# A tuned attention and two-layer kernel: three more quarters of the first layer by seven products, an order written out, and wider fillers

## The chip, the cores and the metric

The kernel runs on one core of a Trainium2 chip. A core has a matrix engine (PE, with its weight loads, PEld), VectorE (DVE), ScalarE (ACT), GpSimd (POOL) and a queue engine (SP) that only issues transfers. Each engine runs its instructions in the order in which they were written; across engines they wait for one another by semaphores. The metric is device time in microseconds (us), lower is better.

## The reference

Attention in chunks of 64 tokens over 8 batches, 8 heads, 576 tokens and 64 dimensions a head, then two layers over the 4608 tokens with a leaky rectifier in between:

```python
scores = scale * np.matmul(q_c, k_c.transpose(0, 1, 2, 4, 3))   # chunks of 64 x 64
scores = scores - np.max(scores, axis=-1, keepdims=True)
attn = np.exp(scores)
attn = attn / (np.sum(attn, axis=-1, keepdims=True) + 1e-09)
out = np.matmul(attn, v_c)
x = out.transpose(0, 2, 1, 3).reshape(4608, 512)
h = x @ w_in                      # 512 x 2048
g = np.maximum(0.01 * h, h)
return (g @ w_out).astype(np.float32)   # 2048 x 512
```

## The kernel before

Tokens go through attention in 36 groups u of 128 tokens (two chunks for all heads). The steps of a group, by the letter that names them in the code:

- `arrive`: POOL issues the loads of q and k, which cast to f16 on the way (`load_rows`, L93).
- `t`: from group 10 on SP issues transposes of q and k by DMA (L428, L431), and POOL copies q into its place QZ, in two halves (`p`, L444). Before group 10 PE transposes them (`pe_t`, L404, L409).
- `s`: PE multiplies q and k (tile Sp, L451). `m`, `b`: DVE takes the maximum and subtracts it. `x`: ACT takes the exponential (L471). `z`, `n`: DVE sums, and DVE or POOL divides (tile en, L487).
- `d`: SP issues the transpose of en by DMA (tile et, L506). In the groups below 8 and in a few others PE transposes it (`e`, L495) and DVE or ACT copies it (`d2`).
- `v`: PE multiplies et by v (tile xp, L517). `a`: ACT copies xp into xT (L530).

The two layers work on 12 blocks of tokens, four of 128 and eight of 512 (`BLOCKS`). In the last eight the second layer is done by Strassen's scheme as Winograd has it: seven products of half size in place of eight, steps `m2` (tiles oA, oB, oC, L371), with sums made by DVE (`sf`, `wf`). In blocks 6 to 11 so is part of the first layer, counted in quarters of a block: `FAST` says how many of a block's four quarters. A quarter by seven products is the PE steps `f` with numbers 1 to 7 (`in_product`, L323, tiles hA, hB, hC), sums of the inputs on DVE (`xf`, tile XF, once for a block), three copies on ACT (`d`, `u2`, `u3`, L199), two additions on DVE (`+u2`, `+u3`, L235) and four activations on ACT (`g..`, L196). A plain quarter is 32 matmuls (`mm1`, L185, tile hT) and four activations on ACT. In blocks 6 and 7 the scheme works on 256 tokens at a time (`UNIT`), so that its matmuls are of 128 columns; in blocks 8 to 11 on 512 with 256 columns.

The order of all steps is made while the program is built. `run()` is a list scheduler: at each point it takes, of the steps that can begin soonest by its own account of durations, latencies, DMA queues, PSUM banks and temporary tiles, the one with the lowest key. `TUNE` shifts the keys of single steps, and `ON` says which engine does a step that several could. Where PE would stand idle ahead of a step in the first 40 us, `run()` puts fillers in, matmuls whose results nobody reads (`idle`, L532): each 128 columns of the identity with itself.

The first q and k come over the queues of SP and ACT as f32 (tiles q_f and k_f) and are cast by DVE and ACT (`cast_q`, `cast_k`). All other loads are issued by POOL, in the order of `front()` and of the groups; POOL makes the identity behind its first loads.

The lines that call the two functions in question:

```python
    second_fast(LAST, place)
    run()
```

## Time and profile before

| | |
|---|---|
| time, median of 3 runs | 277.74 us (276.58 to 278.91) |
| span of the profiled execution | 273.8 us (the page gives no other time of it) |
| matmuls hT, 256 and 128 columns | 96 and 768 |
| matmuls of seven products, first layer | 784 |
| fillers | 86 |

The page's timeline rows read: start and length in us, engine, line, operation, tile written and tiles read, shapes, count, and in brackets the idle time just ahead and what ended it. A group's row has its count, then busy time and the mean of one in ns, then the idle time ahead of them. A row of stretches has from and to, the length, and busy time of PE, PEld, DVE, ACT and POOL with the number of instructions, then the clock, the DMA share and GB/s. Where matmuls follow one another their rows overlap, since a matmul's end is modelled; what one costs is seen from the start of the next. A line "DMA to landing" gives the least, the median and the greatest time from issue to landing of the transfers in the stretch that was asked for.

### The profile page before, as it was taken

What the parts mean: (1) busy time and instruction counts of PE and PEld (TensorE: products, weight loads), DVE (VectorE), ACT (ScalarE), POOL (GpSimd) and SP (SyncE); (2) the same over time, 40 slices, a digit from 0 to 9 for tenths busy, and PEclk for the clock granted to TensorE, in tenths of its full rate; (3) what the DMA queues carried; (4) which work ended last, traced back from release to release, by engine and by line L of the source; (5) the groups of instructions that cost most, each with busy time, mean ns of one, the idle gap of its engine ahead of it and who ended that gap; (6) DMA issues with size and microseconds to landing.
All of it is one profiled execution on the core that took longest, in us unless ns stands there. A gap on an engine that the chain in (4) does not pass through costs nothing.

```text
span 273.8 us, 8229 instructions
## 1 busy us (share of the span) xinstructions
PE 263.2 (96%) x3406; PEld 238.2 (87%) x3406; DVE 208.2 (76%) x375; ACT 193.9 (71%) x359; POOL 158.9 (58%) x198
## 2 busy tenths in 40 slices
PE   1999999999999999999999999999999999999995
PEld 1889578799999999999999999899999989888884
DVE  5895285789978898899788999897879865831671
ACT  6588947778475644999796369978866896378721
POOL 8999783967898959587758778657351000000000
PEclk9999999999999999999999999999999999999999
DMA  9999999999999999999999999999954100220233
GB/s 134 154 191 183 182 176 176 155 173 217 151 158 152 120 143 208 170 144 234 154 155 121 136 140 247 133 186 197 136 84 151 43 19 2 77 79 0 79 115 116
DMA packets 162004, 38.27 MB, mean 140 GB/s; under 512 B 153008, under 2 KB 157616, under 8 KB 161968
## 3 DMA queue, kind: packets, MB, share of 16 engines
q0 software_dynamic: 114384, 18.09, 97.0%
q1 hardware_dynamic: 46544, 19.41, 42.2%
q8 instruction: 26, 0.43, 0.6%
q10 hardware_dynamic: 1040, 0.26, 0.4%
q14 instruction: 10, 0.08, 0.2%
HBM read 36.70 MB, written 9.44 MB: 169 GB/s over the span
## 4 chain that ended last, share of the span: by engine, by line
PE 90%; ACT 3%; DMA 3%; POOL 2%; issue 1%; DVE 0%; POOLq 0%
PE oA L371 20%; PE hT L185 17%; PE hA L323 14%; PE oC L371 10%; PE hC L323 7%; PE oP L210 5%; PE oB L371 5%; PE hB L323 3%; PE Sp L451 3%; PE xp L517 3%; DMA q_in<-in_q_dram 3%; PE tpe L495 1%; PE idle L535 1%; ACT gT L196 1%; ACT xT L530 1%; PE qp L404 1%
## 5 line engine op out<-in xcount | busy, mean ns | idle before, releaser
L371 PEld LDWEIGHTS <-gT 128*128 128x128 f16 x640 | 61.1, 98 | 6.6
L185 PE MATMUL hT<-xT,w_inT 128*128 128x128 f16 (+1 forms) x864 | 58.6, 225 | 0.1
L185 PEld LDWEIGHTS <-w_inT 128*128 128x128 f16 x864 | 53.1, 98 | 2.0 <-issue 0.4
L444 POOL COPY QZ<-QT 64x512 f16<-64x512 f16 x52 | 36.6, 705 | 20.0 <-DMA QT<-q_in 13.1
L196 ACT ACTIVATE gT<-hT 128x512 f16<-128x512 f32 x60 | 35.1, 599 | 15.9 <-PE hT L185 15.6
L235 DVE TENSOR_TENSOR tmp<-hC,tmp 128x512 f32<-128x512 f32 x42 | 27.9, 678 | 16.6 <-PE hC L323 8.3
L487 POOL TENSOR_TENSOR en<-ex,zi 128x512 f16<-128x512 f16 x22 | 23.8, 1083 | 26.8 <-DVE zi L481 12.3
L323 PEld LDWEIGHTS <-VF 128*128 128x128 f16 x448 | 34.5, 98 | 2.4
L93 POOL DMA_DIRECT2D q_in<-in_q_dram x39 | 33.8, 871 | 4.5 <-DMA w_outT<-in_moe_w_out_dram 1.8
L93 POOL DMA_DIRECT2D k_in<-in_k_dram x39 | 33.5, 863 | 1.2 <-DMA VB<-in_v_dram 0.8
L461 DVE TENSOR_REDUCE mx<-Sp 128x8 f32<-128x512 f32 x36 | 24.6, 684 | 10.3 <-PE Sp L451 10.2
L371 PE MATMUL oA<-WF,gT 128*128 128x256 f16 x256 | 32.2, 273 | 0.0
L199 ACT ACTIVATE tmp<-hA 128x512 f32<-128x512 f32 x42 | 24.3, 602 | 6.8 <-PE hA L323 6.8
L196 ACT ACTIVATE gT<-tmp 128x512 f16<-128x512 f32 x42 | 26.4, 634 | 3.7 <-DVE tmp L235 3.6
L323 PEld LDWEIGHTS <-w_inT 128*128 128x128 f16 x336 | 26.2, 98 | 1.9
L471 ACT ACTIVATE ex<-sh 128x512 f16<-128x512 f32 x36 | 22.8, 633 | 7.0 <-DVE sh L465 6.8
L371 PEld LDWEIGHTS <-S 128*128 128x128 f16 x256 | 24.6, 98 | 2.8
L477 DVE TENSOR_REDUCE z<-ex 128x8 f32<-128x512 f16 x36 | 24.3, 676 | 3.3 <-ACT ex L471 3.2
L530 ACT ACTIVATE xT<-xp 128x512 f16<-128x512 f32 x36 | 21.4, 597 | 7.6 <-PE xp L517 7.4
L465 DVE TENSOR_TENSOR sh<-Sp,mx 128x512 f32<-128x512 f32 x36 | 24.5, 681 | 0.6
L323 PE MATMUL hA<-XF,VF 128*128 128x128 f16 (+1 forms) x224 | 24.7, 246 | 0.0
L199 ACT ACTIVATE tmp<-oA 128x512 f32<-128x512 f32 (+1 forms) x27 | 14.9, 552 | 11.7 <-PE oA L371 11.6
(76 smaller groups left out, 478.7 us busy)
## 6 DMA issues: line engine op xcount, KB each, us to landing
out_dram<-osb SPq DMA_DIRECT2D x14, 512.0 KB, 5.2
VB<-in_v_dram POOLq DMA_DIRECT2D x14, 288.0 KB, 9.1
q_in<-in_q_dram POOLq DMA_DIRECT2D x31, 128.0 KB, 8.3
k_in<-in_k_dram POOLq DMA_DIRECT2D x31, 128.0 KB, 8.4
w_inT<-in_moe_w_in_dram POOLq DMA_DIRECT2D x8, 256.0 KB, 7.5
w_outT<-in_moe_w_out_dram POOLq DMA_DIRECT2D x4, 512.0 KB, 9.0
out_dram<-osb SPq DMA_DIRECT2D x6, 256.0 KB, 5.5
v_t<-in_v_dram POOLq DMA_DIRECT2D x4, 128.0 KB, 7.0
```

The source lines that it names most:

```text
L93: nc.gpsimd.dma_start(out=t[a - u * G:z - u * G], in_=src[b, :, r:r + z - a, :].rearrange("h p d -> p h d"))
L185: nc.tensor.matmul(out=hT[:, i, :], lhsT=w_inT[:, t, fc * 128:(fc + 1) * 128], rhs=xT[:, t, r0 % RING:r0 % RING + tb], start=(i == 0 and t ...
L196: nc.scalar.activation(out=to, in_=of, func=AFT.Prelu, bias=0.0, scale=1.0, alpha=0.01)
L199: nc.scalar.activation(out=to, in_=of, func=AFT.Copy, bias=0.0, scale=1.0)
L235: (nc.vector if e == "dve" else nc.gpsimd).tensor_tensor(out=to, in0=a, in1=b, op=ALU.add)
L323: nc.tensor.matmul(out=PA[key][:, c, :], lhsT=w[:, t, fc * 128:(fc + 1) * 128], rhs=x[:, t, :], start=(m in (1, 5) and c == 0 and t == 0), ...
L371: nc.tensor.matmul(out=to, lhsT=lhs[:, fc, p * 128:(p + 1) * 128], rhs=rhs[:, fc, :], start=(fresh and fc == 0), stop=(fc == HB - 1), skip ...
L444: nc.gpsimd.tensor_copy(out=QZ[u % NQZ][part, :, :, s, :], in_=QT[u][part].rearrange("p i (e t) -> p i e t", e=2))
L461: nc.vector.tensor_reduce(out=MX[u], in_=SP[u], axis=AXL.X, op=ALU.max)
L465: nc.vector.tensor_tensor(out=SH[u], in0=SP.pop(u), in1=MX.pop(u).unsqueeze(2).to_broadcast((128, 8, CH)), op=ALU.subtract)
L477: nc.vector.tensor_reduce(out=z, in_=E[u], axis=AXL.X, op=ALU.add)
L530: nc.scalar.activation(out=xT[:, :, at:at + G], in_=xp, func=AFT.Copy, bias=0.0, scale=1.0)
```

## The change

Four things:

1. `FAST` goes from 4, 3, 4, 2, 4, 4 to 4 in each of blocks 6 to 11: 24 quarters of the first layer by seven products instead of 21. The three are one of block 7 and two of block 9.
2. The scheduler goes. In its place `ORDER` lists all 1406 steps by number, with the fillers ahead of a step (how many, in which bank) and the PSUM banks and temporary tiles that the step takes. `TUNE` goes with it. The first third of the list is the order that the scheduler made (113 steps on PE, 98 on ACT, 95 on DVE and 84 on POOL, with the same fillers' places for the most part); behind it the order is another on every engine.
3. `ON` is written out for all steps. Three divisions `n` change engines: group 23 from POOL to DVE, 28 and 33 from DVE to POOL.
4. Fillers are of 512 columns on a tile of ones. DVE sets the tile (a part of XF, which is not yet in use) ahead of everything else that it does. In units of 128 columns there are 112 in place of 86. 21 of them stand ahead of PE's first step now.

```diff
-    FAST = {6: 4, 7: 3, 8: 4, 9: 2, 10: 4, 11: 4}
+    FAST = {6: 4, 7: 4, 8: 4, 9: 4, 10: 4, 11: 4}
...
+    ones = XF[0][:, 0].rearrange("p t n -> p (t n)")
+    nc.vector.memset(ones, 1.0)
     one = sbp.tile([128, 1], FP16, name="one")
     nc.vector.memset(one, 0.0)
...
     def idle(n, tag):
-        t = bank([128, 4, 128], "idle", tag)
-        for i in range(n):
-            nc.tensor.matmul(out=t[:, i % 4, :], lhsT=ident, rhs=ident, start=True, stop=True)
+        t = bank([128, 512], "idle", tag)
+        while n:
+            w = min(n, 4) * 128
+            nc.tensor.matmul(out=t[:, :w], lhsT=ones[:, :128], rhs=ones[:, :w], start=True, stop=True)
+            n -= w // 128
...
     def run():
-        now = {e: 0.0 for e in LAT}
-        now.update(pe=3.8, act=2.6, dve=0.95, pool=1.2, sp=1.3)
...
-        return order
+        for i, fill, *slots in ORDER:
+            s = steps[i]
+            if fill:
+                idle(fill[0], BANKS[fill[1]])
+            for h, slot in zip(s.take, slots):
+                h.slot = BANKS[slot] if h.pool == "bank" else slot
             s.emit()
...
-    TUNE = {('v', 5): (-8, 0.5), ('e', 6): (2, 0.5), ('a', 4): (0, 0.3), ('arrive', 26, 0): (4, 0.8),
...
+    ORDER = [
+        (55, 0), (0, 0), (56, 0), (62, 0), (1, 0), (59, 0), (60, 0), (64, 0), (61, 0), (2, 0), (57, 0), (63, 0), (65, 0), (3, 0), (66, 0), (4, 0), (52, 0), (5, 0),
+        (54, 0), (53, 0), (6, 0), (86, (21, 0), 0), (83, 0, 1), (7, 0), (87, 0), (112, 0, 2), (84, 0), (115, 0, 3), (8, 0), (114, 0), (85, 0), (113, 0), (116, 0),
...
```

The estimates of how long the weights' loads take (`load` in `front()`) change too; with the order written out, no instruction depends on them.

The fillers on PE, in units of 128 columns: before, 4 ahead of Sp of group 0, 40 and 8 ahead of the transposes of q of groups 2 and 3, 15 ahead of Sp of group 2, 19 ahead of the transpose of en of group 1. Now 21 ahead of the first step, 3 ahead of Sp of group 0, 36 and 7 ahead of the same transposes of q, 7 ahead of the transpose of en of group 0, 23 ahead of that of group 1, 9 and 6 ahead of xp of groups 0 and 1.

Two places show how the order moves. ACT around 82 to 91 us, before: ex are the exponentials of groups 13, 14 and 15, xT<-xp is the copy behind xp of group 11, gT<-hT are activations of block 5.

```order
L471 ACTIVATE ex_1890<-sh_1870 128x512
L196 ACTIVATE gT_1631<-hT_1873 128x4x128
L196 ACTIVATE gT_1631<-hT_1902 128x4x128
L196 ACTIVATE gT_1631<-hT_1923 128x4x128
L196 ACTIVATE gT_1631<-hT_1948 128x4x128
L471 ACTIVATE ex_1984<-sh_1968 128x512
L199 ACTIVATE tmp_2010<-oA_1970 128x512
L530 ACTIVATE xT_68<-xp_2014 128x4x128
L471 ACTIVATE ex_2063<-sh_2037 128x512
```

ACT at the same place now, from the exponential of group 13 to that of group 15:

```order
L473 ACTIVATE ex_1842<-sh_1820 128x512
L198 ACTIVATE gT_1578<-hT_1844 128x4x128
L198 ACTIVATE gT_1578<-hT_1868 128x4x128
L198 ACTIVATE gT_1578<-hT_1899 128x4x128
L532 ACTIVATE xT_68<-xp_1923 128x4x128
L198 ACTIVATE gT_1578<-hT_1933 128x4x128
L473 ACTIVATE ex_2021<-sh_1995 128x512
L198 ACTIVATE gT_1578<-hT_2000 128x4x128
L473 ACTIVATE ex_2049<-sh_2017 128x512
```

The copy behind xp of group 11 stands ahead of the fourth activation and of the exponential of group 14 now, as xp itself stands earlier on PE.

POOL from 166 to 177 us, before: q_in_3662 takes q of groups 32 and 33, q_in_3835 that of 34 and 35; QZ<-QT_3536 are the two copies of q of group 29 and QZ<-QT_3640 those of group 30, en are divisions.

```order
L93 DMA q_in_3662<-in_q_dram 128x8x64
L93 DMA k_in_3681<-in_k_dram 128x8x64
L93 DMA q_in_3662<-in_q_dram 128x8x64
L93 DMA k_in_3726<-in_k_dram 128x8x64
L444 COPY QZ_65<-QT_3536 64x8x64
L487 TENSOR_TENSOR en_3777<-ex_3633,zi_3749 128x512
L444 COPY QZ_65<-QT_3536 64x8x64
L487 TENSOR_TENSOR en_3807<-ex_3724,zi_3775 128x512
L93 DMA q_in_3835<-in_q_dram 128x8x64
L444 COPY QZ_65<-QT_3640 64x8x64 x2
```

POOL at the same place now: q_in_3831 takes q of groups 32 and 33, q_in_3568 (whose first half was loaded earlier) that of 34 and 35; QT_3577, QT_3658 and QT_3696 are groups 29, 30 and 31.

```order
L93 DMA k_in_3671<-in_k_dram 128x8x64
L446 COPY QZ_65<-QT_3577 64x8x64 x2
L489 TENSOR_TENSOR en_3735<-ex_3619,zi_3713 128x512
L489 TENSOR_TENSOR en_3788<-ex_3701,zi_3761 128x512
L446 COPY QZ_65<-QT_3658 64x8x64 x2
L93 DMA q_in_3831<-in_q_dram 128x8x64
L489 TENSOR_TENSOR en_3845<-ex_3786,zi_3808 128x512
L446 COPY QZ_65<-QT_3696 64x8x64
L489 TENSOR_TENSOR en_3933<-ex_3864,zi_3889 128x512
L446 COPY QZ_65<-QT_3696 64x8x64
L93 DMA q_in_3831<-in_q_dram 128x8x64
L93 DMA q_in_3568<-in_q_dram 128x8x64
```

The loads of q of groups 32 and 33 stand behind the copies of groups 30 and 31 now; those of k stay ahead of the copies of group 29.

On SP the store of one half of block 6's output stood ahead of the transpose of en of group 26 and stands behind it now. On PE three groups of eight hT matmuls of block 9 and one of product 3 of block 7 (tile oC) stood between the transpose of en of group 27 and xp of group 26 and are gone or behind it; and the sums `xf` of block 9 need the products of block 8 to be done, as they did before.

More of the change, by code (lines that the diff above doesn't have):

```diff
@@ L846, in front @@
                 for m in range(2):
-                    load(("Q", n[0], m), 0.62, lambda a=n[0], m=m: load_w_in(a, m), 1750 if n[0] == 0 else 1580)
+                    load(("Q", n[0], m), 0.62, lambda a=n[0], m=m: load_w_in(a, m), 1560)
             else:
                 load(("P", n[0]), 1.0, lambda a=n[0]: load_w_out(a), 2930)
-        for n, more in ((1, 500), (4, 700)) if arrivals[0].name[0] != "Q" else ((0, 1300), (1, -200)):
-            arrivals[n].dmas = [(p + more / len(arrivals[n].dmas), y) for p, y in arrivals[n].dmas]
         for x in arrivals:
```

182 lines of the change are left out of this document (11 added, 171 removed), and 108 rows, old and new, of tables (ON, ORDER).

## The prediction

> **What bounds the kernel now.** I read the page's busy shares and its chain first, then the waits of TensorE (PE), then busy time by stretch, and last the timeline of the places that the change touches.
>
> ```profile
> span 273.8 us, 8229 instructions
> PE 263.2 (96%) x3406; PEld 238.2 (87%) x3406; DVE 208.2 (76%) x375; ACT 193.9 (71%) x359; POOL 158.9 (58%) x198
> ...
> PE 90%; ACT 3%; DMA 3%; POOL 2%; issue 1%; DVE 0%; POOLq 0%
> ```
> ```profile
> PE kp L409 <- POOL ident masks.py:199: 6.0, 1, 6.0
> PE qp L404 <- DMA q_in<-in_q_dram: 0.4, 1, 0.4
> PE tpe L495 <- ACT gT L196: 0.3, 1, 0.3
> PE xp L517 <- POOL VB L120: 0.2, 1, 0.2
> ```
> ```profile
> 18.35:270.45 252.10, 251.62 (x3246) 227.45 (x3242) 193.99 (x342) 181.74 (x337) 142.27 (x171) 1.00 1.41 139
> ```
> The waits are all that PE ever waited for; their columns are the total, the times and the longest. Three of the four end before 18.35 us. From there to the last matmul PE is idle for 252.10 - 251.62 = 0.48 us. So the time is the point where PE's dense work begins, plus its own work, plus a tail. A change can win by giving PE less work or an earlier start, and any wait that it puts into the dense stretch is paid in full. The span is 273.8 us and the page gives no time beside it; the median of the runs, 277.74, is 3.9 above it. I take these 3.9 as unchanged and make the sum on the median.
>
> **The three quarters.** The work itself, from the chain (start, time, what):
>
> ```profile
> 107.84 0.89 PE hA L323 x16
> ...
> 127.14 0.87 PE hT L185 x8
> ```
> A matmul of 256 columns costs 0.87/8 = 0.109 us, one of 128 costs 0.89/16 = 0.0556. A plain quarter of the first layer is 32 matmuls of 256 columns, 3.48 us. As seven products it is 28 of 256 columns in block 9 (3.05 us) and 56 of 128 in block 7 (3.12 us), whose unit is 256 tokens. Two quarters of block 9 and one of block 7 change: 3 x 3.48 = 10.44 goes, 2 x 3.05 + 3.12 = 9.22 comes. PE has 1.2 us less to do, all of it on the path. That is the first term: -1.2.
>
> Each changed quarter also has seven copies and activations on ScalarE (ACT) in place of four, and two more additions on VectorE (DVE):
>
> ```profile
> L196 ACT ACTIVATE gT<-hT 128x512 f16<-128x512 f32 x60 | 35.1, 599 | 15.9 <-PE hT L185 15.6
> ...
> L235 DVE TENSOR_TENSOR tmp<-hC,tmp 128x512 f32<-128x512 f32 x42 | 27.9, 678 | 16.6 <-PE hC L323 8.3 <-ACT tmp L199 8.3
> L196 ACT ACTIVATE gT<-tmp 128x512 f16<-128x512 f32 x42 | 26.4, 634 | 3.7 <-DVE tmp L235 3.6
> ...
> L199 ACT ACTIVATE hB<-hA 128x512 f32<-128x512 f32 x21 | 12.0, 588 | 8.0 <-PE hA L323 7.7
> ```
> ```profile
> 117.00:139.00 22.00, 22.00 (x351) 21.02 (x349) 19.63 (x40) 20.11 (x39) 16.68 (x21) 1.00 1.86 175
> ...
> 169.00:196.00 27.00, 27.00 (x307) 24.46 (x305) 23.68 (x44) 23.70 (x45) 15.96 (x20) 1.00 1.90 181
> ```
> Four evictions of 599 ns are 2.4 us, seven of 588 to 634 are 4.1 to 4.4: ACT gains 1.9 us a quarter, DVE 2 x 0.68 = 1.4. Around block 7 (first row; the columns after PE and its weight loads are DVE, ACT, POOL) ACT goes from 20.1 to 22.0 of 22 us. Around block 9 it goes from 23.7 to 27.4, in a stretch that shrinks from 27 to 26.1. There ACT has 1.3 us too much, which must lie over into the next block. The copies for which PE waits (d, u2, u3) can run ahead of the activations that nobody needs yet, so I book zero, and keep +1.3 for the range. That is also what it costs if the cover is gone. What two operations win there isn't excluded, but PE was idle for nothing there, so there is no gain below zero.
>
> **The fillers and the front.** The first 113 PE steps, up to about 81 us, and those of ACT, DVE and POOL beside them, keep their order; only the fillers differ.
>
> ```profile
> 3.29 0.48 DVE L555 MEMSET QZ<- 128x512 uint32 x1
> ...
> 4.63 0.43 DVE L538 CAST q_in<-q_f 128x512 f16<-128x512 f32 x1 [0.86 <-DMA q_f<-in_q_dram]
> ```
> ```profile
> 9.66 3.11 PE L535 MATMUL idle<-ident 128*128 128x128 f16 x40
> 13.12 0.40 PE L404 MATMUL qp<-ident,q_in 128*128 128x128 f16 x4 [0.35 <-DMA q_in<-in_q_dram]
> ...
> 14.46 1.00 PE L535 MATMUL idle<-ident 128*128 128x128 f16 x15
> ...
> 15.75 1.23 PE L535 MATMUL idle<-ident 128*128 128x128 f16 x19
> ...
> 18.11 0.41 PE L517 MATMUL xp<-et,VB 128*128 128x64 f16 x8 [0.24 <-POOL VB L120]
> ```
> ```profile
> 16.79 1.27 POOL L120 COPY VB<-v_t 64x256 f16<-64x256 f16 x3
> ```
> The memset of the ones is no longer than the 0.48 us of the one shown; DVE waits 0.86 us for the first q right behind it, so it is hidden, and costs that rest if the q came earlier. Fillers are counted in 128 columns: 86 before, 112 now. The first 21 run while PE waited for the identity (the 6.0 us among the waits). The 36 ahead of the landing of q at 13.1 us are 4 fewer. Between there and 18.35 stand 52 against 42, about 52 x 0.0556 = 2.9 us by the warm rate. Where do they end? The last xp before the dense work waits for POOL's copies of v, 16.79 + 1.27 = 18.06, and no order on POOL changes there. The 10 more units cost 0.6 us, and about as much goes because Sp of group 2 has no fillers ahead of it any more. So the dense start stays at 18.35: term zero. Bounds: -0.5, all idle time of the dense stretch, and +0.6, the added units if POOL's cover went.
>
> What clock do these matmuls have? The 40 fillers run 3.11/40 = 0.078 us apiece, between 0.0556 and about twice that, and the 15 at 14.46 already 0.067 with the drain. PE reaches its full rate among the 40. The Trainium skill ("TensorE: Matmul & The Clock Gate", Part 1) says that the array runs at half clock until about 3.4 us of sustained work, counted in a window that runs freely, and Part 4 adds that transposes don't count as work. By that rule the early fillers, some 2 us and then a wait, need not open the gate by themselves; the trace agrees in that PE, begun at 5.96 with transposes, was slow until it had run fillers for a while.
>
> **The new order behind 81 us.** Three places are tight: where PE takes the transposed weights of attention (xp), or q (Sp), sooner than before.
>
> ```profile
> 82.37 1.19 SPq L506 DMA_TRANSPOSE et<-en  x1
> ...
> DMA to landing us min/median/max: 7.0/7.0/7.0
> ...
> 90.68 0.40 PE L517 MATMUL xp<-et,VB 128*128 128x64 f16 x8
> ```
> First, xp of group 11. Its transpose is issued at 82.4 and lands 7.0 later, at 89.4; its POOL step and all ahead of that keep their place, and ahead of it on SP only two transposes change places. One group of 16 hT matmuls (0.89) and one of 8 oA (0.87) that stood ahead of xp now stand behind it: PE is there 1.76 us earlier, at 88.9. Behind it on PE waits everything. That is a new wait of 0.5 us, the second term: +0.5 (bounds 0, if the transpose gets through faster, and 1.0).
>
> ```profile
> 172.75 7.05 SPq L506 DMA_TRANSPOSE et<-en  x2
> ...
> DMA to landing us min/median/max: 8.8/8.8/8.8
> ...
> 183.34 0.40 PE L517 MATMUL xp<-et,VB 128*128 128x64 f16 x8
> ```
> Second, xp of group 26: its transpose lands at 172.75 + 8.8 = 181.6. Three hT groups and one oC group (4 x 0.87) that stood ahead of it are gone or behind it, and with what block 7 saved PE is there 3.9 us earlier, at 179.5. Left alone that is 2.1 us of waiting. But the normalisation of this group stands earlier on DVE, and an output store that was ahead of the transpose on SP now stands behind it. I book zero and keep +2.1: a wait at one such place pushes the later ones back and isn't added to theirs, so the +0.5 of group 11 is inside it.
>
> ```profile
> 165.92 0.95 POOL L93 DMA_DIRECT2D q_in<-in_q_dram  x1
> ...
> 175.47 1.27 POOL L444 COPY QZ<-QT 64x512 f16<-64x512 f16 x2
> ...
> 183.76 0.94 POOL L93 DMA_DIRECT2D q_in<-in_q_dram  x1
> ...
> DMA to landing us min/median/max: 10.0/11.6/12.6
> ...
> DMA to landing us min/median/max: 5.3/5.3/5.3
> ...
> DMA to landing us min/median/max: 5.9/5.9/5.9
> ...
> 193.90 0.40 PE L451 MATMUL Sp<-KT,QZ 128*128 128x64 f16 x8
> ```
> Third, Sp of group 32, at 193.9 and now 1.25 us earlier, 192.65. The load of its q was issued at 165.9; now POOL issues it behind the copies of group 30, which end at 176.7. From there: the load, 5.3 (issued alone, as the one at 183.8 was, the second landing row) to 10.0 (least of the burst of four from 165.9, the first), the transpose, 5.9 (its own, the third) to 8.8 (the one of group 26), and POOL's copies, 1.3. That is 189.2 to 196.8, so from 3.4 us to spare to 4.1 late. The load is now nearer to the one issued alone, so I book zero.
>
> The tail is the same products of the last block in nearly the same order: zero. Sum: 277.74 - 1.2 + 0.5 = 277.0 us.
>
> **The rivals.**
> - Late weights. Group 26 keeps the landing of before, and PE waits 2.1 us in place of 0.5: 277.74 - 1.2 + 2.1 = 278.6. For it: the transposes of the row above take 7 to 8.8 us, and xp moved earlier than its supply at several groups. Against it: what stands ahead of it was moved too. ACT's 1.3 us too much around block 9 would give 277.8 and lies on the way to it.
> - Slower by q of group 32. With 10.0 and 8.8 PE waits 4.1 us: 277.74 - 1.2 + 4.1 = 280.6. It decides from 14.65 us for load and transpose together; each us above that is lost.
> - Nothing waits, and the last 0.5 us of idle time goes too: 277.74 - 1.2 - 0.5 = 276.0. For it: counted in the two orders, PE has 0.87 us of other work or more between any product and the next one that needs its copy, the shortest that before has too.
> - The clock comes late: the array stays at half rate past 13.1 us, because the first fillers are followed by a wait. Worked out from rows, at twice 0.0556: 52 units are 5.8 us, eight groups of four such are 3.6, so dense work begins at 22.5 instead of 18.35: 277.74 - 1.2 + 4.1 = 280.6. Against it: before reached the full rate by 13 us with less work ahead. (The Trainium skill's rule above, of "TensorE: Matmul & The Clock Gate", is what would do it.)
>
> **How the numbers follow.** The forecast, 277.0, gets 0.54 (its own range 276.2 to 277.9); late weights 0.18, q of group 32 0.14 (from 278.7 to 280.6), nothing waits 0.10, the clock 0.04. One measurement of this kernel tells about 1% from no change (the runs lie from 276.58 to 278.91): under 274.96 is faster, over 280.52 slower. Even the best case ends within 1%; only the scatter of the runs, 1.2 below the median, gets it under: 0.05. Slower takes most of the clock, half of q and a little of late weights: 0.13. The rest, 0.82, is within 1%. The range goes from the best case less that scatter, 274.9, to 279.7, the middle of the q case; about 0.17 lies outside.
>
> **What would show it.** Matmuls hT fall from 864 to 768, idle from 86 to 31. The last xp ahead of dense work still waits for POOL, and dense work begins by 18.4. PE's waits show xp at about 89 with half a microsecond on SP's transpose, and no Sp beyond 190 that waits for QZ. ACT is over 98% busy around block 7. Wrong would be: waits of PE on ACT in blocks 7 or 9, dense work that begins past 19, or PE's idle time in the dense stretch over 2 us.

## The result and the profile after

| | before | after |
|---|---|---|
| time, median | 277.71 us (275.08 to 280.17, 20 runs) | 278.50 us (277.29 to 282.67, 20 runs) |
| ratio to before | | 1.0053 [1.0028, 1.0078] |
| span of the profiled execution | 273.8 us | 276.0 us (its time 277.82) |

The change makes the kernel slower by half a per cent. Here and below a ratio leaves out executions that took over 1.5% more than the fastest of their kernel, while a median is of all, so the two can differ. It is worth being clear at once about two executions that are not alike: the span of 276.0 us belongs to a time of 277.82, 1.8 us more than the span. By the same 1.8 the execution of before with its span of 273.8 took about 275.6, two microseconds under the median of its kernel. The trace that the prediction was worked out from is one of the quickest of before. The spans on record say the same without this estimate: of the 154 executions of before that ran beside the experiments, the median span is 275.9 us, and nine are at 273.8 or less.

The page of after, first the busy times by engine, then the shares of the chain that ended last:

```profile
span 276.0 us, 8186 instructions
...
PE 264.9 (96%) x3367; PEld 234.4 (85%) x3367; DVE 214.4 (78%) x381; ACT 197.0 (71%) x368; POOL 157.3 (57%) x199
...
PE 83%; DMA 8%; ACT 3%; DVE 2%; POOL 2%; issue 1%; DVEq 0%; POOLq 0%
```

PE carries the chain as before, but DMA has 8% of it. The waits of PE in after (what PE waited in and the line, what for; total, times, longest in us); the first two and that of qp end ahead of the dense stretch:

```profile
PE kp L411 <- POOL ident masks.py:199: 2.1, 1, 2.1
PE idle L538 <- DVE zeros L157: 1.5, 1, 1.5
PE xp L519 <- DMA et<-en: 1.0, 1, 1.0
PE qp L406 <- DMA q_in<-in_q_dram: 0.9, 1, 0.9
PE hA L325 <- DVE XF L285: 0.4, 1, 0.4
PE tpe L497 <- ACT gT L198: 0.3, 1, 0.3
PE Sp L453 <- DMA KT<-k_in: 0.3, 1, 0.3
PE hC L325 <- ACT gT L198: 0.2, 1, 0.2
```

The stretches of after, with the columns that were explained for before:

```profile
18.35:82.00 63.65, 63.32 (x985) 54.97 (x982) 47.02 (x85) 47.57 (x85) 50.37 (x62) 1.00 1.98 171
82.00:117.00 35.00, 33.47 (x483) 31.03 (x482) 30.62 (x51) 19.65 (x37) 24.84 (x32) 1.00 1.95 161
117.00:139.00 22.00, 21.59 (x361) 20.56 (x357) 21.20 (x43) 20.16 (x39) 13.99 (x17) 1.00 1.95 170
139.00:169.00 30.00, 29.93 (x387) 27.58 (x385) 27.73 (x46) 21.00 (x40) 24.39 (x30) 1.00 2.29 146
169.00:196.00 27.00, 27.00 (x311) 24.29 (x310) 24.39 (x47) 24.84 (x49) 15.62 (x20) 1.00 1.47 163
196.00:272.00 76.00, 76.00 (x754) 68.25 (x750) 48.83 (x79) 51.52 (x100) 11.02 (x14) 1.00 0.35 79
```

PE stands idle for 1.53 us between 82 and 117 (35.00 against 33.47) and for 0.41 between 117 and 139. The largest piece is xp of group 14, which asks 1.75 us sooner in PE's work than before, while its weights are divided later (on DVE a sum for the second layer, a sum of the weights and all of group 15 come first) and SP sends group 15's transpose ahead of it. The view by tile of et between 96 and 108 us shows the two transposes, 15 at 97.5 and 14 at 98.8, the wait of 1.0, and the time from issue to landing:

```profile
L508 SPq DMA_TRANSPOSE et<-en x2: 1254/1547/1840, 97.5 to 98.8; - x2
...
  DMA et<-en: 1.0, 1
...
DMA to landing us min/median/max: 7.7/7.9/8.0
```

To put every profile of this study on one scale, the span is cut in four. Dense: from the start to the first matmul of the dense work. Work: all matmuls from there on, by the distance from one start to the next where nothing waits, 29.4, 55.6, 109.1 and 215.5 ns for 64, 128, 256 and 512 columns. Waits: what the distances between starts have above that, each over 15 ns. Rest: the remainder, nearly all of it behind the last matmul.

| profile | span | dense | work | waits | rest |
|---|---|---|---|---|---|
| before, the one shown | 273.8 | 18.35 | 250.38 | 1.23 | 3.81 |
| before, again (`b_again`) | 274.2 | 18.47 | 250.38 | 1.56 | 3.79 |
| after | 276.0 | 18.37 | 249.13 | 4.18 | 4.29 |
| after, again (`a_again`) | 277.1 | 18.58 | 249.13 | 5.15 | 4.27 |

So from the one shown to after: -1.25 of work, as forecast, +0.02 of the front, +2.95 of waits and +0.48 at the end, together +2.2 us. The waits are the term to explain: before's trace had 1.23, and the time of an ordinary run of before leaves room for 3.3 (277.7 less 1.8 is a span of 275.9, less 18.37, 250.38 and 3.8).

### The profile page after: what moved, and what is told of

Same layout as the page of the kernel before. It is cut to its first block, busy times and chain, and to the rows that moved or that the text cites. A ratio compares the mean times of both kernels' runs of the same rounds, so it can differ in the third digit from the quotient of the medians.

```text
span 276.0 us, 8186 instructions
## 1 busy us (share of the span) xinstructions
PE 264.9 (96%) x3367; PEld 234.4 (85%) x3367; DVE 214.4 (78%) x381; ACT 197.0 (71%) x368; POOL 157.3 (57%) x199
## 2 busy tenths in 40 slices
DMA packets 162005, 38.28 MB, mean 139 GB/s; under 512 B 153008, under 2 KB 157616, under 8 KB 161968
## 4 chain that ended last, share of the span: by engine, by line
PE 83%; DMA 8%; ACT 3%; DVE 2%; POOL 2%; issue 1%; DVEq 0%; POOLq 0%
PE oA L373 18%; PE hA L325 14%; PE hT L187 14%; PE oC L373 9%; PE hC L325 7%; DMA et<-en 5%; PE oP L212 5%; PE oB L373 4%; PE hB L325 3%; PE xp L519 3%; PE Sp L453 3%; DMA q_in<-in_q_dram 2%; PE tpe L497 1%; ACT gT L198 1%; PE idle L538 1%; POOL q_in L93 1%
## 5 line engine op out<-in xcount | busy, mean ns | idle before, releaser
L446 POOL COPY QZ<-QT 64x512 f16<-64x512 f16 x52 | 34.5, 665 | 28.7 <-DMA QT<-q_in 21.2
L187 PE MATMUL hT<-xT,w_inT 128*128 128x128 f16 x768 | 47.1, 219 | 0.0
L237 DVE TENSOR_TENSOR tmp<-hC,tmp 128x512 f32<-128x512 f32 x48 | 32.3, 684 | 15.9 <-ACT tmp L201 8.9
L187 PEld LDWEIGHTS <-w_inT 128*128 128x128 f16 x768 | 44.0, 98 | 0.6
L325 PEld LDWEIGHTS <-VF 128*128 128x128 f16 x512 | 39.9, 98 | 3.7 <-issue 0.9
L198 ACT ACTIVATE gT<-hT 128x512 f16<-128x512 f32 x48 | 27.9, 600 | 14.2 <-PE hT L187 14.0
L489 POOL TENSOR_TENSOR en<-ex,zi 128x512 f16<-128x512 f16 x23 | 24.6, 1068 | 20.1 <-ACT tmp L201 10.6
L201 ACT ACTIVATE tmp<-hA 128x512 f32<-128x512 f32 x48 | 28.1, 601 | 6.9 <-PE hA L325 6.6
L325 PEld LDWEIGHTS <-w_inT 128*128 128x128 f16 x384 | 30.3, 98 | 2.2
L198 ACT ACTIVATE gT<-tmp 128x512 f16<-128x512 f32 x48 | 29.9, 633 | 2.6 <-DVE tmp L237 2.6
L325 PE MATMUL hA<-XF,VF 128*128 128x128 f16 (+1 forms) x256 | 28.3, 246 | 0.4 <-DVE XF L285 0.4
```

Of the source, the lines that this page charges most:

```text
L187: nc.tensor.matmul(out=hT[:, i, :], lhsT=w_inT[:, t, fc * 128:(fc + 1) * 128], rhs=xT[:, t, r0 % RING:r0 % RING + tb], start=(i == 0 and t ...
L198: nc.scalar.activation(out=to, in_=of, func=AFT.Prelu, bias=0.0, scale=1.0, alpha=0.01)
L201: nc.scalar.activation(out=to, in_=of, func=AFT.Copy, bias=0.0, scale=1.0)
L237: (nc.vector if e == "dve" else nc.gpsimd).tensor_tensor(out=to, in0=a, in1=b, op=ALU.add)
L325: nc.tensor.matmul(out=PA[key][:, c, :], lhsT=w[:, t, fc * 128:(fc + 1) * 128], rhs=x[:, t, :], start=(m in (1, 5) and c == 0 and t == 0), ...
L446: nc.gpsimd.tensor_copy(out=QZ[u % NQZ][part, :, :, s, :], in_=QT[u][part].rearrange("p i (e t) -> p i e t", e=2))
```

## The experiments

Eighteen kernels, in five batches; each batch has its own runs of before on the same chip, and ratios are to those. The theories, as the expectations number them:

- T1: the new order loses the time, at places where PE takes transposed data sooner.
- T2: the three quarters load DVE and ACT so that PE waits for them, whatever the order.
- T3: the fillers cost it.
- T4: the execution of before that was profiled was a lucky one.
- T5: fewer filler instructions shift the fetches of PE's program, and the gaps that they make in DMA traffic, against the loads.
- T6: DMA supply is a second bound up to 200 us, so that PE work taken out comes back as waits.
- T7: Sp of group 32 is the floor of all that stands ahead of it.
- T9: dense work follows the landing of q by a chain, with the new fillers in it.

### The parts of the change apart

**`b_again`**: the kernel before, nothing edited.

> The kernel before, unchanged, profiled a second time. Ratio to before by every theory: 1.000, and what it differs from that is the noise of the comparison. T4 (the profiled execution of before was a lucky one): the span is 275 to 276 us instead of 273.8, and the excess gaps on PE behind 18.3 us add up to 3 to 4 us instead of 1.5, most of them at xp whose transposed weights landed only 1 to 2.5 us ahead of their use. T1 (the loss is the new order): the span is again near 274 and the gaps stay under 2 us.

Measured: 276.85 us (275.33 to 281.34, 12 runs), ratio 0.9979 [0.9944, 1.0014]. The profile has a span of 274.2 and 1.56 us of waits: by this profile alone T4 would fall. Its time is 276.14, though, again under the median of its own runs. A profile shows one execution, and a second one does not show the spread. The 154 spans above do: T4 holds for the execution that the prediction was made from.

**`b_24`**: only the number of quarters.

```diff
-    FAST = {6: 4, 7: 3, 8: 4, 9: 2, 10: 4, 11: 4}
+    FAST = {6: 4, 7: 4, 8: 4, 9: 4, 10: 4, 11: 4}
```

> Only the number of quarters by seven products is changed (24 instead of 21); the order is the one that before's scheduler finds for that, the fillers are those of before. T1 (the loss of the change is its written order): PE has 1.2 us less work and no wait of its own at groups 14, 16, 20, 21, so 1.0 us faster, ratio 0.995 to 0.998. T2 (the three quarters load ACT and DVE in blocks 7 and 9 so that PE waits there, whatever the order): ratio 1.002 to 1.006, and PE waits in blocks 7 and 9 for DVE's sums or ACT's copies, 1 us or more in all. T3 (fillers): ratio as by T1.

Measured: 281.94 us, ratio 1.0147 [1.0113, 1.0182]: worse than T2 has it. The work is 249.13, so the 1.25 us are gone here too, but the waits are 6.03, 4.9 of them between 150 and 215 us. The largest in its profile are

```profile
PE hA L323 <- DVE XF L283: 1.7, 1, 1.7
PE oC L371 <- ACT xT L530: 0.9, 1, 0.9
PE hB L323 <- ACT hB L199: 0.7, 1, 0.7
```

With the scheduler's own order the three quarters do what T2 says: PE waits for DVE's sums of x and for ACT's copies. The written order of the change puts these away (its own wait for XF is 0.4), and with its new fillers the changed kernel is about a per cent quicker than `b_24`.

**`b_fill`**: only the fillers, ones in place of the identity, up to 512 columns each, and 21 units more at the start.

> Only the fillers are changed: ones instead of the identity, up to 512 columns each, and 21 more units at the start. T1 and T2: dense work begins at 18.3 to 18.4, ratio 0.999 to 1.001. T3 (the fillers cost the time): ratio 1.002 to 1.006, with dense work later than 18.5 or a lower granted clock behind it.

Measured: 279.32 us (275.27 to 284.14) against 277.89 in its batch, ratio 0.9976 [0.992, 1.0032]; the two point in different ways, since the ratio leaves out five of the twelve executions, and it stays unclear. Dense work begins at 18.41, as T1 and T2 had it. But the profile, of the same order as before, has 4.74 us of waits, at xp, Sp and tpe between 110 and 190 us. The order of before waits too, in some executions.

**`a_d14`**: the changed kernel, group 14 ahead of group 15 again, as before had it. Here and below a step is its letter and its group, with /0 for q and /1 for k; sf, m2, mm1, f and save have the block and then the part.

```diff
 DVE:
-    z13 m14 m15 sf4/2 vf3 b14 b15 z14 z15 n15 n14
+    z13 m14 b14 m15 vf3 b15 z14 sf4/2 n14 z15 n15
 SP:
-    d15 d14 t18/1
+    d14 t18/1 d15
```

> The changed kernel, with the order of before on DVE around group 14 (b and n of group 14 ahead of the weight sums and of group 15's) and on SP (d of group 14 ahead of that of 15). T1: xp of group 14 no longer waits its 1.2 us at about 107; 0.5 to 1.2 us faster than the changed kernel, ratio to before 1.001 to 1.003. If waits further on take it back (each pushes the next ones back): 1.004 to 1.005 as the changed kernel. T2 and T3: 1.005, no different from the changed kernel.

Measured: 278.85 us, ratio 1.0002 [0.9964, 1.0041], which allows every theory. Its profile tells more: xp of group 14 waits 0.25 instead of 1.2, and Sp of group 21 0.74 instead of 0.2; span 276.3. So about half of the wait that was taken away came back behind it: 3.69 us of waits in all against 4.18 in after. That the span is no shorter comes from the front, where dense work began only at 19.16 us in this execution.

### The fetches of PE's program

The profiles of the first batch divide by their DMA: with the old fillers KT's transposes between 40 and 120 us took 7.0 and 6.8 us at the median, with the new ones 7.8 to 8.8. The trace also holds the packets that bring PE's program, 16 KB in about 1 us each, roughly one for every 128 matmuls. They come at 51.1, 62.2, 67.6, 75.7 and 83.4 us in before, at 58.0, 65.1, 70.4, 79.8 and 88.8 in after, which has 55 filler matmuls fewer. Behind some of them all DMA traffic stops for a moment. Two stretches of 2 us, in forty slices each, after from 57.5 to 59.5 us:

```profile
GB/s 151 143 154 115 118 110 123 115 149 466 126 148 146 143 156 126 139 159 123 138 159 151 125 105 100 64 69 62 79 49 33 41 46 20 15 8 10 5 10 13
...
q8 instruction: 1, 0.02, 3.7%
```

and before from 67 to 69 us:

```profile
GB/s 276 292 276 302 300 143 105 105 161 161 161 464 149 139 139 146 141 143 143 149 141 143 149 159 190 213 269 254 269 246 259 202 212 216 198 61 31 13 8 10
...
q8 instruction: 1, 0.02, 3.4%
```

In both a fetch (the row of q8) begins about 0.5 us behind the stretch's start, and some 0.7 to 1.1 us later the traffic falls from 150 and more towards 10 GB/s. Does this phase set the time? Three kernels move it, with the same filler work cut into more matmuls, beside after once more.

**`a_again`**: after, nothing edited. **`a_p86`**, **`a_p59`**: after with narrower fillers (SAVE is 53 in `a_p59`). **`bf_p86`**: `b_fill` with them (SAVE is 21).

```diff
+    SAVE = [26]
     def idle(n, tag):
         t = bank([128, 512], "idle", tag)
         while n:
-            w = min(n, 4) * 128
+            w = min(n, 4, SAVE[0] + 1) * 128
+            SAVE[0] -= w // 128 - 1
```

> The changed kernel, unchanged, profiled a second time beside the others. All theories: ratio to before 1.003 to 1.008, excess gaps on PE behind 18.3 us of 3.5 to 5 us. T5 (the fewer filler instructions shift PE's instruction fetches, and the gaps in DMA traffic behind them, against the loads and transposes): fetches of PE's program again near 58, 65, 70.5, 80 and 89 us, the loads up to 86 us again 0.3 MB behind those of before (10.9 against 11.2 MB), KT's transposes at a median near 7.9 us between 40 and 120 us instead of 7.0.

> The changed kernel with the same 112 units of fillers, but cut into 86 matmuls (as many as before has) instead of 31, so that every later matmul has the number that it had in before. T5: fetches of PE's program back near 51, 62, 67.5, 75.5, 83.5 us, loads and transposes of 40 to 120 us as quick as in before (KT 7.0, et 6.3, k_in 8.9 us), the waits at groups 14 to 21 down to 0.5 to 2 us; 1.5 to 3 us faster than the changed kernel, ratio to before 0.993 to 0.999. T1 (the new order alone): the same waits as the changed kernel, 1.003 to 1.008. T2 (the quarters' load on ACT and DVE): 1.003 to 1.008.

> As the one with 86, but with 59 matmuls of fillers: half way between. T5: fetches half way too (about 54, 63, 69, 78, 86 us, or one period off), and a time of its own, not tied to the changed kernel's: anywhere from 0.993 to 1.010. T1 and T2: 1.003 to 1.008, no different from the changed kernel.

> The kernel before with the new fillers (ones, 21 units more at the start), cut so that they are 86 matmuls again instead of 37. T5: loads and transposes as quick as in before, gaps on PE behind 18.3 us back from 5.1 to 1.5 to 2 us, ratio 0.997 to 1.001. T3 (the fillers slow the DMA in another way, by the work or the memory that they use): loads and transposes as late as with 37, gaps of 4 to 5 us, ratio 1.003 to 1.008.

(`b_fill` has 28 filler matmuls, not the 37 of the last expectation.)

| | filler matmuls | median | ratio | KT to landing | waits |
|---|---|---|---|---|---|
| `a_again` | 31 | 278.97 | 1.0035 [1.0002, 1.0068] | 8.0 | 5.15 |
| `a_p59` | 59 | 280.72 | 1.0092 [1.0050, 1.0134] | 6.9 | 4.41 |
| `a_p86` | 86 | 281.53 | 1.0098 [1.0060, 1.0137] | 7.0 | |
| `bf_p86` | 86 | 277.73 | 0.9989 [0.9951, 1.0027] | 7.6 | 3.19 |

(`a_p86` has no waits in the table, since its profiled execution took 284.0 us, far above its median; `a_p59`'s took 278.1, 2.6 us under its own.) The fetches moved as forecast, to 50.8, 62.1, 68.1 and 76.7 us in `bf_p86`. In all seven profiles with 31 or 28 filler matmuls and full loads in the first three batches and of after, traffic falls under 60 GB/s at some point between 58.5 and 60.75 us, in none of the six with 86. And the changed kernel's time does hang on the number of fillers, but against T5's sign: bringing the phase of before back makes it slower by a further half per cent, although its transposes become quicker. So T5 is not the cause of the rise. How the time comes to hang on it is not shown. That the written order is fitted to its own count of instructions is only argued, and the transposes do not follow the phase alone: `b_cut1` and `b_pe` below, with the 86 fillers of before, have KT at 8.1 and 8.0 us. T3 has nothing for it in `bf_p86`.

### Easing the order, and taking work out of before

**`a_early`**: xp and Sp of the tight groups later on PE, with `a_d14`'s edit.

```diff
 PE, each moved behind the step named:
+    v11: mm1 5/2/2    s16: m2 4/3/0    v14: f6/0/1/6    v15: m2 5/7/0
+    s21: m2 6/1/0     v19: f7/0/0/5    v20: f7/0/0/3    v21: s24
```

**`a_q32`**: group 32 supplied sooner. **`a_both`**: both.

```diff
 SP:   d26, then
-    d28 t31/1 save6/1 save7/1 t32/1 t32/0
+    t31/1 t32/1 t32/0 d28 save6/1 save7/1
 POOL: load of q32 ahead of that of k32, p32 ahead of n30, p33 ahead of n31
```

**`b_cut1`**: before, with 1.3 us of PE work taken out.

```diff
     def mm1(j, a, h, tag):
+                n = tb // 2 if j in (7, 9) and t == NT - 1 else tb
                 nc.tensor.matmul(
-                    out=hT[:, i, :],
+                    out=hT[:, i, :n],
-                    rhs=xT[:, t, r0 % RING:r0 % RING + tb],
+                    rhs=xT[:, t, r0 % RING:r0 % RING + n],
```

> The changed kernel with its tight places between 88 and 150 us eased: on PE xp of groups 11, 14, 15, 19, 20, 21 and Sp of groups 16 and 21 stand 0.4 to 1.3 us of other work later, and group 14 comes ahead of 15 again on DVE and SP. T1 (these places are the loss): the waits there fall from some 3 us to under 1, and the time by 1.5 to 2.5 us; ratio to before 0.996 to 0.999. T7 (the floor is Sp of group 32, whose q is ready only at 195.3 us in the changed kernel because SP holds its transposes behind that of group 28's weights): the waits go, but PE then waits 1.5 to 3 us for QZ at Sp of group 32; 1.002 to 1.007, no better than the changed kernel.

> The changed kernel with group 32 (and 31, 33) supplied sooner: the load of q of 32 ahead of that of its k on POOL, its two transposes and that of k of 31 ahead of the weights of group 28 on SP, POOL's copies of q for 32 and 33 ahead of the normalisations of 30 and 31. T1: the waits at groups 11 to 21 stay, so no better than the changed kernel, 1.003 to 1.007; q of group 32 is ready by 188 us instead of 195.3. T7 alone (the only floor): 1 to 3 us faster, 0.994 to 1.000.

> Both edits together. T1 and T7 in series (either one alone gives nothing or little, since the other takes it): 2 to 3 us faster than the changed kernel, ratio to before 0.992 to 0.998, with under 1.5 us of excess gaps on PE behind 18.3 us. T6 (supply as a whole, DMA that is busy through to 200 us, sets the time of everything ahead of Sp of group 33, and PE's work there doesn't count): new waits of 2 to 3 us elsewhere ahead of 200 us, 1.002 to 1.007.

> The kernel before with 1.3 us of PE work taken out where the change takes it out, and nothing else: in the plain quarters of blocks 7 and 9 the last of the four row tiles of x multiplies half its columns (24 matmuls of 128 instead of 256 columns; half of those sums lack a quarter of their terms). The same instructions in the same order, so the same fetches. T1, T7: the order of before has the room for it: 1.0 to 1.3 us faster, 0.995 to 0.997. T6: new waits take it back, 0.999 to 1.001.

| | median | ratio | span | work | waits |
|---|---|---|---|---|---|
| `a_early` | 279.68 | 1.0050 [1.0012, 1.0088] | 278.7 | 249.13 | 6.88 |
| `a_q32` | 278.83 | 1.0042 [1.0003, 1.0081] | 277.5 | 249.13 | 5.00 |
| `a_both` | 279.19 | 1.0059 [1.0022, 1.0095] | 276.4 | 249.13 | 3.87 |
| `b_cut1` | 277.85 | 0.9990 [0.9950, 1.0030] | 276.9 | 249.09 | 5.93 |

None of the three gains anything. In `a_q32` POOL ends its copies of q for group 32 at 191.6 us (two copies of 3.24 us that begin at 188.35) where after has 195.3, so the edit did what it says, and T7 falls as the only floor. In `a_early` the waits at groups 14, 16 and 21 go, but xp of group 11 still waits 0.8 us, and others come: Sp waits 1.7 us for KT at 172 us, and oA 1.2 us for ACT's copies at 109, a wait that the edit itself made. T1 and T7 in series would have made `a_both` the quickest kernel of all. It is not.

The run that asks T6 most directly is `b_cut1`. The same order, the same instructions, 1.29 us less work, and no gain that can be told from none: 277.85 against 277.91 in the same batch. But the lower end of its interval, 0.9950, would still hold all of the 1.29 us, so it does not decide alone. Its waits:

```profile
PE Sp L452 <- DMA KT<-k_in: 1.5, 2, 0.8
PE tpe L496 <- POOL en L488: 1.2, 1, 1.2
...
PE Sp L452 <- ACT gT L197: 0.3, 1, 0.3
```

In the order of before, with PE as quick as after makes it, PE waits for the transposes of k, as T6 has it. That the cut made these waits is not shown, since `b_fill` waits 4.74 us with all of PE's work. (The longest wait, for POOL, is at 118 us, ahead of the work that was taken out; it belongs to an execution with slow loads, as the 8.1 us of its KT transposes show.)

### DMA supply

Six of the fourteen loads of v bring 288 KB each between 40 and 120 us. With a quarter of the rows from the third sequence on there is some 2.6 MB less to move, and PE, ACT, DVE and SP do the same work in the same order (attention then takes old values of v for the rest). POOL has less to do as well: issuing the loads of v takes it 10.3 us in `b_light` and 16.3 in before.

```diff
     def load_v(b, m, c0, c1):
+        n = CH if b < 2 else CH // 4
         nc.gpsimd.dma_start(
-            out=VB[b % NVB][m * CH:(m + 1) * CH, :, :, m * CH:(m + 1) * CH].rearrange("p h c d -> p (h c) d"),
-            in_=v[b, m * H // 2:(m + 1) * H // 2].rearrange("h (c j) d -> j (h c) d", j=CH),
+            out=VB[b % NVB][m * CH:m * CH + n, :, :, m * CH:(m + 1) * CH].rearrange("p h c d -> p (h c) d"),
+            in_=v[b, m * H // 2:(m + 1) * H // 2].rearrange("h (c j) d -> j (h c) d", j=CH)[:n],
```

**`b_light`**: before with it. **`b_light_cut`**: `b_light` with the edit of `b_cut1`. **`a_light`**: after with it.

> The kernel before with less DMA traffic and nothing else: of each load of v from the third sequence on only a quarter of the rows (so attention takes old values of v for the rest); some 2.6 MB less behind 50 us. T6 (supply by DMA, busy through to 200 us, is the second bound): transposes and loads are quicker, the waits of PE behind 18.3 us fall to 1.0 to 1.5 us in every run, and the scatter of the runs with them; 1.5 to 3 us faster, ratio to before 0.989 to 0.995. T1: 0.997 to 1.001.

> The same with the 1.3 us of PE work taken out as well (the last row tile of x multiplies half its columns in the plain quarters of blocks 7 and 9). T6: with the traffic gone the PE work counts again: 1.0 to 1.3 us faster than with the lighter loads alone, 0.004 to 0.005 below it. If PE's work doesn't count for another reason (an engine other than DMA): no difference between the two.

> The changed kernel with the same lighter loads of v. T6: its waits fall to 1 to 2 us, and it is faster than the kernel before with the same loads by the 1.25 us of PE work less the 0.45 us that it takes longer behind its last store: 0.5 to 1.0 us, 0.002 to 0.004 below it. T1 (its order costs the time whatever the supply): slower than the kernel before with the same loads, by 0.003 to 0.006, with the waits at groups 11, 14, 16 and 21 still there.

| | median | lowest to highest | ratio | dense | work | waits | rest |
|---|---|---|---|---|---|---|---|
| `b_light` | 276.03 | 275.42 to 277.04 (12 runs) | 0.9945 [0.9915, 0.9975] | 18.56 | 250.38 | 0.95 | 3.84 |
| `b_light_cut` | 274.05 | 273.81 to 274.94 (6 runs) | 0.9893 [0.9853, 0.9933] | 18.67 | 249.09 | 0.87 | 3.84 |
| `a_light` | 275.91 | 275.23 to 278.41 (12 runs) | 0.9963 [0.9931, 0.9995] | 19.30 | 249.13 | 1.23 | 4.25 |

Transposes by SP between 40 and 120 us, count and median time to landing, in before:

```profile
QT<-q_in SPq DMA_TRANSPOSE x13, 7.6
KT<-k_in SPq DMA_TRANSPOSE x12, 7.0
et<-en SPq DMA_TRANSPOSE x8, 6.3
```

in after:

```profile
QT<-q_in SPq DMA_TRANSPOSE x13, 8.1
KT<-k_in SPq DMA_TRANSPOSE x12, 7.9
et<-en SPq DMA_TRANSPOSE x8, 7.6
```

and in `b_light`, with the list of all of PE's waits below them:

```profile
QT<-q_in SPq DMA_TRANSPOSE x13, 5.4
KT<-k_in SPq DMA_TRANSPOSE x12, 5.7
et<-en SPq DMA_TRANSPOSE x8, 5.1
```

```profile
PE kp L410 <- POOL ident masks.py:199: 6.1, 1, 6.1
PE qp L405 <- DMA q_in<-in_q_dram: 1.2, 1, 1.2
PE xp L518 <- POOL VB L121: 0.4, 1, 0.4
PE tpe L496 <- ACT gT L197: 0.3, 1, 0.3
```

With less to move, the kernel before is 1.8 us faster (276.03 against 277.84), the waits for transposes are gone, and the runs of `b_light` lie within 1.6 us instead of 4.2 for before in the same batch. Now PE's work counts: `b_light_cut` lies wholly under `b_light`, by 2.0 us in the medians of the times, 1.65 in those of the spans and 1.2 in the two profiles (273.7 and 272.5), where 1.29 were taken out. Under full loads `b_cut1`'s interval allows at most 1.4 us of gain, and the two medians lie above that. So the same cut is worth more under light loads than under full ones, as T6 says; that it is worth nothing under full ones is not shown.

That it was DMA that was relieved, and not POOL, is in part argued. The times from issue to landing above, in which POOL has no part, fall by 1.2 to 2.2 us against before; no run made POOL quicker alone.

`a_light` refutes the last part of my expectation, and T1 as it is put there, whatever the supply. Its places at groups 11, 14, 16 and 21 don't wait any more in this profile, and yet it equals `b_light` (275.91 and 276.03) where 0.5 to 1.0 us of gain were forecast. For the two profiles the table says why: -1.25 of work, +0.28 of waits, +0.41 of rest and +0.74 of the front. One profile is not the last word here either: `a_front_light` below, of the same order on the same loads, waits 2.54 us, 0.94 of them at xp of group 11.

Whether the new order costs time under full loads stays open. After and `b_cut1` have the same amount of PE work, and the ratios 1.0053 and 0.9990 lie some 1.7 us apart; the front and the end, below, are 0.95 of that.

### The front

From the first matmul behind q's landing (qp of group 2) to the dense work takes 5.77 us in after, and 5.75 to 5.93 in all nine profiles with its front; 5.20 to 5.75 in the nine with that of before, 5.35 in the mean against 5.83. Ten units of fillers more stand in between, which the prediction had costed at nothing.

**`a_front_light`**, **`a_front`**: ten units fewer, on the light and on the full loads. **`b_pe`**: before, with the transposes of two more groups on PE.

```diff
-    (123, (23, 3), 3)   ...   (96, (9, 5), 5)
+    (123, (16, 3), 3)   ...   (96, (6, 5), 5)
```

```diff
-    BY_PE = [8, 9, 18, 27, 29, 31]
+    BY_PE = [8, 9, 14, 18, 21, 27, 29, 31]
```

> The changed kernel with the lighter loads of v and 10 units of fillers fewer between the landing of q and the dense work (16 and 6 in place of 23 and 9; before had that many fewer). T9 (the dense work begins a fixed chain behind q's landing, 5.75 to 5.93 us in all nine profiles of the new fillers, 5.2 to 5.75 with the old ones): the chain is 5.2 to 5.35 us and the kernel 0.4 to 0.6 us faster than with the lighter loads alone, 0.0015 to 0.002 below it. As the prediction had it (POOL's copies of v end the wait, the fillers are hidden): the chain stays near 5.8 us when q lands early, and no difference.

> The same with all loads. T9: dense work 5.2 to 5.4 us behind q. T6: the 0.5 us that the front gains are mostly lost again to later supply, since nothing of the DMA traffic starts sooner: 0 to 0.5 us faster than the changed kernel, ratio to before 1.001 to 1.005.

> A version that might beat both: the kernel before with the weights of attention of two more groups, 14 and 21, transposed on PE in place of the DMA (2 x 4 transposes of 128 columns, 0.45 us more PE work; its scheduler then finds its own order). T6: two DMA transposes of 6 to 8 us fewer where supply is tight, the waits behind 80 us fall by 0.5 to 1.5 us; net 0.2 to 1.0 us faster, 0.996 to 0.999. If its own order is less well tuned, as with the 24 quarters: 1.002 to 1.015.

Measured: `a_front_light` 276.50 us, ratio 0.9916 [0.9884, 0.9948]; to the before of its batch (278.28) that is 0.9936 in the medians. `a_light` had 0.9931 in the medians and 0.9963 as a ratio, so the two point in different ways and no gain is shown. `a_front` 279.82, 1.0025 [0.9978, 1.0072], which can't be told from after's 1.0053. The chain is 5.68 and 5.75, not 5.2 to 5.35, so T9 as a matter of these ten units falls. What stands there instead, in the timeline of `a_front` (start, length, engine, line, operation, tiles, and the idle time just ahead), with two rows of other engines that the last xp needs:

```profile
16.58 0.39 PE L519 MATMUL xp<-et,VB 128*128 128x64 f16 x8
17.23 0.40 PE L411 MATMUL kp<-ident,k_in 128*128 128x128 f16 x4 [0.26 <-DMA k_in<-in_k_dram]
17.46 0.49 PE L538 MATMUL idle<-XF 128*128 128x512 f16 x2
18.01 0.39 PE L519 MATMUL xp<-et,VB 128*128 128x64 f16 x8
...
16.36 1.36 POOL L120 COPY VB<-v_t 64x256 f16<-64x256 f16 x3
...
17.22 0.41 DVE L120 COPY et<-tpe 128x512 f16<-128x512 f16 x1
```

PE waits for k, which it transposes ahead of the last xp, and behind that come the six units that the change put there, 0.55 us. Before has no fillers at this place. But POOL's copies of v end only at 17.72 and DVE's copy of et at 17.63, so without the six units the last xp could have begun at about 17.75 in place of 18.01. In the nine profiles with after's front all that it needs is ready 0.10 to 0.43 us ahead of it, 0.30 in the mean; with the front of before it is 0.06 at most. By these rows the six units are about half of the 0.5 us. No run took them alone, and the other half is open.

`b_pe`: 279.62, ratio 1.0076 [1.0038, 1.0113]. Fewer transposes by DMA, but its scheduler finds an order that waits for sums of DVE at 159 to 162 and 214 us. No version here beats the kernel before under full loads.

## Why the prediction was wrong

The forecast was 277.0 us and slightly faster; measured are 278.5 and 0.5% slower, inside the range given. The rival nearest in number, late weights at 278.6, is not what happened: it had PE wait 2.1 us at group 26, and PE does not wait there. One of the signs of being wrong came: PE's idle time in the dense stretch is over 2 us (0.33, 1.53, 0.41 and 0.07, or 2.34, by the stretches of after). Point by point:

- **Bound by PE alone.** This is the step that failed: the saving of 1.2 us was entered in the sum in full, against one wait of 0.5. Two things stood behind it. The waits of before, 0.48 us of idle time by the busy times of its trace (1.23 by the distances of starts), were taken as those of the kernel; yet of the 3.9 us between this span and the median only some 1.8 lie outside a span, and the other two would be waits of an ordinary execution that this trace did not have. And the row of the DMA share, busy up to 200 us, was not read as a bound. The runs show in its place that the same saving gains nothing that can be told from none under full loads (`b_cut1`, 0.9990, at most 1.4 us), and 1.65 to 2.0 us when there is less to move (`b_light_cut`). This step is not the whole miss: of the 1.5 us between forecast and measurement the front and the end, both booked at zero, are 0.95, and the rest, some 0.6, are waits beyond the 0.5 that was booked.
- **PE's work, -1.2.** Right: 250.38 to 249.13, with hT at 768 matmuls and the fillers at 31 as forecast.
- **The dense start, term zero.** Right in the one profile (18.37), wrong as a term: +0.5 us in the mean of nine profiles (18.83 against 18.36), near the bound of +0.6 that was kept. The row that was read (xp waits 0.24 us for POOL) was true, but in after xp does not wait for POOL. The fillers added behind k are about half of the 0.5 us by the rows; the other half is open.
- **The clock.** Right that it isn't late.
- **Group 11, +0.5.** Right place, asked at 88.97; it waited 0.15, and 0.15 to 0.9 in the other profiles of this order.
- **Groups 26 and 32.** Right to book zero: neither waits in after, 32 with 0.4 us to spare (q ready at 195.3, Sp at 195.6). In `a_again` it waits 0.66. Had PE come 3 us sooner it would have waited there; `a_q32` supplied this q sooner for no gain.
- **Only three tight places.** Wrong. The waits came at groups 14, 16 and 21 and at XF of block 7, since many xp of before had only 1.3 to 2.5 us between the landing of their transpose and their use, and xp of 14, 15, 20 and 21 ask 1.8 to 3.7 us sooner. Easing these places gained nothing, so under T6 they say where the time is lost, not why.
- **ACT and DVE around block 9, zero.** Right for this order (PE loses 0.07 us from 139 to 169, and around block 7 ACT is busy for 20.16 of 22 us, not for over 98%). In the scheduler's own order, `b_24`, that load and the order cost 1.5% together.
- **The tail, zero.** Wrong by +0.45: from the last store's landing to the end the twelve profiles with 24 quarters take 1.6 us and seven of the eight with 21 take 1.2, with the same last products. The eighth, `b_pe`, takes 1.43, so the number of quarters is not all of it. What sets this time is not resolved.

Summed over ordinary executions: -1.25 of work, +0.5 of the front, +0.45 of the end, and waits that rise by about 1.1 (what is left to the measured +0.8, and not measured by itself). In the pair of profiles with lighter loads the waits rise by 0.3 instead, and the two kernels are equal.

## What to carry to other kernels

An engine that is busy 96% of the time is not the only bound if another resource is busy for the same stretch: take a little work out of the first on purpose (fewer columns, the same instructions) and see whether the time follows, before designing a change that saves such work. A trace is one execution; compare its own time with the median before reading its waits as the kernel's. A written order can depend on things that look harmless: here the same filler work in 86 matmuls instead of 31 cost the changed kernel a further half per cent, so time an order again after every such change.

## What the runs showed of the hardware

- Fetches of PE's program, about 1 us of DMA each for some 128 matmuls, are followed in several places by about a microsecond in which the traffic of all queues falls from some 150 to 10 GB/s (rows above). Changing nothing but the number of filler matmuls from 31 to 86 moved the changed kernel from 1.0035 to 1.0098 of before.
- The same transposes of k took 6.8 to 8.8 us at the median in executions with the same traffic, and the times of before spread over 4 to 6 us in each batch; with 2.6 MB less to move it was 5.5 to 6.3 us. What sets the rate of one execution is open. The view of before's DMA has this row:

```profile
DMA packets 162004, 38.27 MB, mean 140 GB/s; under 512 B 153008, under 2 KB 157616, under 8 KB 161968
```

  The Trainium skill ("DMA: Bandwidth & Descriptors", Specifications) names 512 B as the least transfer for full line rate. Of the packets here 153008 of 162004 are smaller; whether that sets the rate no run here shows, since none changed their size.
- In after the fillers at 9.60 us ran at the full rate at once, nine of 512 columns in 2.11 us, while the last four transposes ahead of them, at 8.74, took 0.41 us to the start of what follows, and four later on take 0.23.
